# Blocks 6 and 7 normalised one by one, the d table's sines after blocks 8 and 9, and the last two blocks normalised after the first gate product

## The chip, the cores and the metric

The kernel runs on one NeuronCore of one Trainium2 chip. The metric is the device time of one execution in microseconds (us). A core has five engines that run their own instruction streams and wait for one another through semaphores: TensorE (PE in the profile, with its weight loads as PEld), VectorE (DVE), ScalarE (ACT), GpSimd (POOL) and SyncE (SP, which here only issues DMAs). Each engine takes its instructions in the order in which they were issued.

## The reference, cut to what matters

```python
def _A_ref(x, w_r, w_i):                       # x: 1 x 2048 x 512
    X = rfft2(x.astype(float32), axes=(-2, -1))
    return irfft2(X * (w_r + 1j * w_i), s=(2048, 512)).astype(bfloat16)

def _B_ref(x, w1, b1, w2, b2):                 # w1: 2048 x 1792, w2: 1792 x 2048
    h = _layernorm(x, axis=-1)
    u = gelu(einsum("bsd,sf->bdf", h, w1) + b1)
    return (einsum("bdf,fs->bds", u, w2) + b2).transpose(0, 2, 1)

g = sigmoid((x * gate_w).sum(-1, keepdims=True))
return g * _A_ref(x, A_w_r, A_w_i) + (1 - g) * _B_ref(x, B_w1, B_b1, B_w2, B_b2)
```

The same x goes into the gate, the spectral branch A and the MLP branch B, whose two products run over the 2048 tokens.

## The kernel before

The 2048 tokens are cut into NB = 16 blocks of 128 rows (block b lies in `xa` for b below 8, in `xb` above). Everything stands in one function; its order is written out by hand and is the order on each engine.

**The first stage.** Each block is normalised over its 512 features into `hn[:, b]`, and as soon as a block is ready TensorE multiplies it by the first 1024 columns of w1 (`mm1`, L275): 8 matmuls of 128x512 per block, one for each group `ft` of 128 columns, summed over the blocks in 8 PSUM banks. Blocks 0 to 11 are multiplied block by block, 8 `ft` each. The last four blocks are taken per `ft`: for the first `ft` blocks 12, 13, 14, 15, then a GELU (L354) on ScalarE, then the next `ft`, and so on. So a block that is late stops TensorE, which holds its matmuls in order.

**The steps of one block's normalisation:**

- `bstat(b)` (L246): bn_stats on DVE.
- `aggr(b0, b1)`: bn_aggr on DVE (L253), then 1e-5 added to the variance (L255), then rstd as a power of -0.5 on POOL (L258). Where `on_dve(b0)` holds (b0 up to NDVE = 6, or 14) L255 runs on DVE; elsewhere it runs on POOL, and POOL also makes the negated mean (L257).
- `norm(b0, b1)`: nmr = -mean * rstd, on DVE (L264) where `on_dve(b0)` holds, elsewhere on POOL (L262); then one ScalarE activation per block writes `hn` (L267).
- `norm_dve(b)` (L271): for blocks 0 to 5 DVE writes `hn` itself, with no nmr.

Blocks 6 and 7 are one pair before the change, as are 8 and 9, 10 and 11, 12 and 13, 14 and 15.

**The tables.** ScalarE also computes sines for the Fourier matrices: `sines_d()` makes the table TD of the feature axis from `md`, three activations (L198 twice, L201); `sines_a(0)` and `sines_a(1)` make TA of the token axis from `ma[0]` and `ma[1]`, four activations and one. Before each of them DVE masks the integer angles (`mask`, L195: 768 columns for md, 1024 for each `ma`). TD and TA go through DMA transposes on SP (L346, L348) and are first read by TensorE in `token` and `dpass` of branch A.

**Beside and after it.** `gprod(q)` (L279) is the gate's product of x and gate_w on DVE, four instructions of 2048 columns; after them DVE goes on with the radix-16 part of branch A's transform (L387 and on), and POOL makes row indices and gathers rows of the spectral weights (L182 to L189, L106). After the first stage TensorE takes the remaining 768 columns of w1 (L458), then w2 (L468), and `fill` deals these matmuls out between the Fourier matmuls of branch A by a clock kept in the program. That order is fixed when the kernel is built.

Of the kernel before, what the change touches and what calls it, by code (L numbers as in the profile page):

```python
# [18 lines left out]
NB = 16  # L19
# [3 lines left out]
NDVE = 6  # L23
# [20 lines left out]
def kernel(  # L44
# [57 lines left out]
    def gather_w(i):  # L102
        w = (A_w_r, A_w_i)[i]
        for o, src, idx in ((wn[:, i, 8:16].rearrange("p e l -> p (e l)"), w.rearrange("(c e) l -> c (e l)", e=8), 0),
                            (wn[:, i, 16], w, 1)):
            nc.gpsimd.indirect_dma_start(out=o, out_offset=None, in_=src,  # L106
                                         in_offset=bass.IndirectOffsetOnAxis(ap=widx[:, idx:idx + 1], axis=0))
# [51 lines left out]
    def iota(dst, pattern, base, cm=0):  # L159
        nc.gpsimd.iota(dst, pattern=pattern, base=base, channel_multiplier=cm,  # L160
                       allow_small_or_imprecise_dtypes=True)
# [19 lines left out]
    def gather_rows():  # L181
        gp = nc.gpsimd  # L182
        iota(widx[:, 0:1], [[0, 1]], 255, -2)
        gp.tensor_scalar(wf[:, 0:1], acol[:, 0:1], 63.5, 1016.0, op0=Alu.is_ge, op1=Alu.mult)
        gp.tensor_scalar(wf[:, 1:2], acol[:, 0:1], 0.5, -1024.0, op0=Alu.is_lt, op1=Alu.mult)
        gp.tensor_scalar(wf[:, 2:3], acol[:, 0:1], -16.0, 2048.0, op0=Alu.mult, op1=Alu.add)
        gp.tensor_add(wf[:, 0:1], wf[:, 0:1], wf[:, 1:2])
        gp.tensor_add(wf[:, 0:1], wf[:, 0:1], wf[:, 2:3])
        gp.tensor_copy(widx[:, 1:2], wf[:, 0:1])  # L189
# [4 lines left out]
    def mask(m, n):  # L194
        nc.vector.tensor_single_scalar(m, m, n - 1, op=Alu.bitwise_and)  # L195

    def nsin(dst, m, n):
        nc.scalar.activation(dst, m, ActF.Sin, bias=c_mpi, scale=2.0 * PI_IN / n)  # L198

    def psin(dst, m, n):  # L200
        nc.scalar.activation(dst, m, ActF.Sin, bias=c_pi, scale=-2.0 * PI_IN / n)  # L201
# [5 lines left out]
    def sines_d():  # L207
        nsin(TD[:, :, 1], md[:, 1], 1024)
        nsin(TD[:, :, 2], md[:, 0], 1024)
        psin(TD[:, :, 0], md[:, 0], 1024)  # L210

    def angles_a(v):
        mask(ma[v][:], 2048)
        if v == 0:
            mask(mc[:], 2048)

    def sines_a(v):
        if v == 1:
            nsin(TA[:, :, 1], ma[1][:], 2048)
        else:  # L220
            nsin(TA[:, :, 2], ma[0][:], 2048)
            psin(TA[:, :, 0], ma[0][:], 2048)
            nsin(TA[:, 0, 2, 0:1], mc[:], 2048)
            psin(TA[:, 0, 0, 0:1], mc[:], 2048)
# [20 lines left out]
    def bstat(b):  # L245
        nc.vector.bn_stats(out=stats[:, b, :], in_=xh[b // 8][:, b % 8, :])  # L246

    def on_dve(b):
        return b <= NDVE or b == NB - 2

    def aggr(b0, b1):
        for b in range(b0, b1):
            nc.vector.bn_aggr(out=mv[:, b, :], in_=stats[:, b, :])  # L253
        eng = nc.vector if on_dve(b0) else nc.gpsimd
        eng.tensor_scalar(mv[:, b0:b1, 1], mv[:, b0:b1, 1], 1e-5, 0.0, op0=Alu.add, op1=Alu.add)  # L255
        if not on_dve(b0):
            nc.gpsimd.tensor_scalar(nmr[:, b0:b1], mv[:, b0:b1, 0], -1.0, 0.0, op0=Alu.mult, op1=Alu.add)  # L257
        nc.gpsimd.tensor_tensor(rstd[:, b0:b1], mv[:, b0:b1, 1], c_mhalf.to_broadcast([P, b1 - b0]), op=Alu.pow)  # L258

    def norm(b0, b1):  # L260
        if not on_dve(b0):
            nc.gpsimd.tensor_mul(nmr[:, b0:b1], nmr[:, b0:b1], rstd[:, b0:b1])  # L262
        else:
            nc.vector.scalar_tensor_tensor(nmr[:, b0:b1], mv[:, b0:b1, 0], -1.0, rstd[:, b0:b1],  # L264
                                           op0=Alu.mult, op1=Alu.mult)
        for b in range(b0, b1):
            nc.scalar.activation(hn[:, b, :], xh[b // 8][:, b % 8, :], ActF.Identity,  # L267
                                 bias=nmr[:, b:b + 1], scale=rstd[:, b:b + 1])

    def norm_dve(b):  # L270
        nc.vector.tensor_scalar(hn[:, b, :], xh[0][:, b, :], mv[:, b, 0:1], rstd[:, b:b + 1],  # L271
                                op0=Alu.subtract, op1=Alu.mult)
# [5 lines left out]
    def gprod(q):  # L278
        nc.vector.tensor_mul(prod[q // 2][:, 4 * (q % 2):4 * (q % 2) + 4],  # L279
                             xh[q // 2][:, 4 * (q % 2):4 * (q % 2) + 4],  # L280
                             gwb[:, None, :].to_broadcast([P, 4, D]))
# [30 lines left out]
    for b in range(2, NDVE):  # L312
        bstat(b + 1)
        norm_dve(b)
        if b + 1 < NDVE:
            aggr(b + 1, b + 2)
    for b in range(NDVE, NB, 2):
        if b > NDVE:
            bstat(b)
        if b == NDVE + 2:  # L320
            norm(b - 2, b)
            sines_d()
        bstat(b + 1)
        aggr(b, b + 2)
        if b == NDVE:
            mask(md[:], 1024)
        if b == NB - 2:
            angles_a(1)
        if b > NDVE:
            norm(b, b + 2)  # L330
        if b == NB - 6:
            angles_a(0)
            sines_a(0)
# [3 lines left out]
            mm1(b, ft)  # L337
    for q in range(4):
        gprod(q)
    gather_rows()  # L340
    gather_w(0)
    gather_w(1)
# [452 lines left out]
    b = NB - 1  # L795
# [36 lines left out]
```

## Time and profile before

| What | us |
|---|---|
| time, median of 3 runs (lowest to highest) | 129.69 (128.85 to 129.98) |
| the profiled execution's own time | 128.63 |
| its span from first to last instruction | 126.7 |
| outside the span, 128.63 - 126.7 | 1.93 |
| PE busy | 122.3 |
| DVE busy | 111.6 |
| ACT busy | 89.7 |
| POOL busy | 39.6 |

The profile is one execution. A line of its timeline gives the start and the length of one instruction, or of several alike in a row (x2), counted in us from the span's start; in brackets the idle time of the engine just before it and what ended that. Two instructions in a row on one engine overlap a little, so the spacing from start to start is what an engine's order costs, and it is shorter than the length that stands there: two `hn` activations in a row are listed at 0.80 us each and start 0.70 us apart.

### The profile page before, as it was taken

Reading aid. Unit: us, or ns where it says so; the run is one execution under the profiler, and the core shown is the slowest. Engines: PE = TensorE matmul, PEld = TensorE weight load, DVE = VectorE, ACT = ScalarE, POOL = GpSimd, SP = SyncE. Lnnn points to the kernel's source line nnn. Section 1 sums busy time; section 2 is a strip of 40 time slices with the busy share of each in tenths; the row PEclk is TensorE's granted clock in tenths of the full one; section 3 lists DMA queues with packets and bytes.
Section 4 is the critical chain, followed back from the end, with each engine's and each line's share of the span. In section 5 each row is a group of like instructions: output and inputs, shape, how many; then the busy total and the mean of one; then the engine's idle time right before and its main releaser. Section 6 shows DMA issues by size and latency. Waiting matters only on the chain.

```text
span 126.7 us, 2074 instructions
## 1 busy us (share of the span) xinstructions
PE 122.3 (97%) x750; PEld 65.2 (51%) x750; DVE 111.6 (88%) x190; ACT 89.7 (71%) x137; POOL 39.6 (31%) x67
## 2 busy tenths in 40 slices
PE   6999999999999999999999999999999999999990
PEld 2244444444444576557764765477644444444480
DVE  4799998999999999999999999999999999993140
ACT  4391299999897699998994799229785599522420
POOL 7133288998887198000040000000000000261200
PEclk9999999999999999999999999999999999999998
DMA  3899999998899999999579206710021101269991
GB/s 95 268 327 379 368 374 352 292 309 262 206 276 121 320 290 293 290 287 291 143 220 294 65 0 190 228 42 0 0 79 50 41 3 41 83 82 201 175 224 29
DMA packets 34635, 24.05 MB, mean 190 GB/s; under 512 B 5536, under 2 KB 32032, under 8 KB 34624
## 3 DMA queue, kind: packets, MB, share of 16 engines
q1 hardware_dynamic: 32516, 21.02, 60.4%
q0 software_dynamic: 1936, 2.76, 13.0%
q8 instruction: 6, 0.10, 0.3%
q10 hardware_dynamic: 172, 0.13, 0.3%
q14 instruction: 5, 0.04, 0.1%
HBM read 19.15 MB, written 3.67 MB: 180 GB/s over the span
## 4 chain that ended last, share of the span: by engine, by line
PE 97%; DVE 0%; issue 0%
PE yb L468 36%; PE u L275 22%; PE u L458 16%; PE ivt L657 5%; PE ivd L673 3%; PE pw L240 3%; PE dp L525 3%; PE yb L800 2%; PE tok L516 2%; PE tok L517 2%; PE ivt L651 0%; PE tok L513 0%; DVE tbv L802 0%; DVE warm L145 0%; PE pb L239 0%
## 5 line engine op out<-in xcount | busy, mean ns | idle before, releaser
L468 PE MATMUL yb<-gl,w2t 128*128 128x512 bf16 x210 | 47.4, 379 | 0.0
L468 PEld LDWEIGHTS <-w2t 128*128 128x128 bf16 x210 | 20.2, 98 | 22.1
L275 PE MATMUL u<-hn,w1a 128*128 128x512 bf16 x128 | 28.5, 385 | 0.0
L458 PE MATMUL u<-hn,w1b 128*128 128x512 bf16 x96 | 23.3, 379 | 0.0
L448 ACT ACTIVATE tbv<-yb,ombb,omg 128x512 bf16<-128x512 f32 x15 | 11.6, 775 | 15.3 <-PE yb L468 15.1
L275 PEld LDWEIGHTS <-w1a 128*128 128x128 bf16 x128 | 12.7, 99 | 15.9 <-issue 1.5
L778 POOL DMA_DIRECT2D out_dram<-ap x3 | 4.0, 1528 | 49.2 <-DVE ap L773 45.3
L458 PEld LDWEIGHTS <-w1b 128*128 128x128 bf16 x96 | 9.0, 98 | 8.0
L286 ACT ACTIVATE junk<-prod 128x512 bf16<-128x512 bf16 x16 | 10.1, 631 | 0.3
L354 ACT ACTIVATE gl<-u,bcol 128x512 bf16<-128x512 f32 x14 | 9.2, 688 | 1.3 <-PE u L458 0.8
L629 ACT CAST R<-ivt 128x1024 bf16<-128x1024 f32 x8 | 7.8, 1038 | 2.3 <-PE ivt L657 2.3
L258 POOL TENSOR_TENSOR rstd<-mv,consts 128x2 f32<-128x2 f32 (+1 forms) x9 | 6.3, 703 | 8.1 <-DVE mv L255 8.0
L629 ACT CAST H<-ivd 128x1024 bf16<-128x1024 f32 x7 | 6.9, 1047 | 0.8 <-PE ivd L673 0.8
L787 DVE TENSOR_TENSOR tbv<-tbv,ap 128x512 bf16<-128x512 bf16 x3 | 1.3, 425 | 5.5 <-ACT tbv L448 5.5
L246 DVE BATCH_NORM_STATS2 stats<-xa 128x6 f32<-128x512 bf16 x8 | 5.5, 686 | 0.5 <-DMA xa<-in_A_x_dram 0.5
L267 ACT ACTIVATE hn<-xb,nmr,rstd 128x512 bf16<-128x512 bf16 x8 | 5.8, 802 | 0.0
L547 DVE TENSOR_TENSOR tatb<-PMA,wn 128x1024 bf16<-128x1024 bf16 x8 | 5.0, 690 | 0.2 <-issue 0.2
L246 DVE BATCH_NORM_STATS2 stats<-xb 128x6 f32<-128x512 bf16 x8 | 5.2, 676 | 0.0
L267 ACT ACTIVATE hn<-xa,nmr,rstd 128x512 bf16<-128x512 bf16 x2 | 1.5, 804 | 5.1 <-DVE nmr L264 5.1
L673 PEld LDWEIGHTS <-R 128*128 128x128 bf16 x64 | 3.8, 98 | 2.5 <-ACT R L629 2.5
L547 DVE TENSOR_TENSOR tatb<-PMB,wn 128x2048 bf16<-128x2048 bf16 x4 | 4.7, 1226 | 0.2
L518 ACT CAST ZA<-tok 128x1024 bf16<-128x1024 f32 x4 | 4.0, 1019 | 1.4 <-PE tok L517 1.3
(198 smaller groups left out, 225.8 us busy)
## 6 DMA issues: line engine op xcount, KB each, us to landing
w2t<-in_B_w_dram SPq DMA_DIRECT2D x8, 896.0 KB, 9.8
w1b<-in_B_w_dram SPq DMA_DIRECT2D x3, 1024.0 KB, 16.3
w1a<-in_B_w_dram SPq DMA_DIRECT2D x2, 1024.0 KB
out_dram<-tbv SPq DMA_DIRECT2D x14, 128.0 KB, 4.0
out_dram<-ap POOLq DMA_DIRECT2D x3, 512.0 KB, 6.8
w1a<-in_B_w_dram SPq DMA_DIRECT2D x4, 256.0 KB, 4.4
w1a<-in_B_w_dram SPq DMA_DIRECT2D x2, 512.0 KB, 8.0
xb<-in_A_x_dram SPq DMA_DIRECT2D x2, 512.0 KB, 7.3
```

The lines of the kernel that those rows point to most:

```text
L246: nc.vector.bn_stats(out=stats[:, b, :], in_=xh[b // 8][:, b % 8, :])
L267: nc.scalar.activation(hn[:, b, :], xh[b // 8][:, b % 8, :], ActF.Identity, bias=nmr[:, b:b + 1], scale=rstd[:, b:b + 1])
L275: nc.tensor.matmul(u1[ft], lhsT=w1a[b // 4][:, b % 4, ft * P:(ft + 1) * P], rhs=hn[:, b, :], start=(b == 0), stop=(b == NB - 1))
L286: nc.scalar.activation(junk[:], prod[b // 8][:, b % 8], ActF.Copy, accum_out=glog[:, b:b + 1])
L354: nc.scalar.activation(gl[:, ft, :], src, ActF.Gelu_apprx_tanh, bias=b1f[:, ft:ft + 1], scale=1.0)
L448: nc.scalar.activation(tbv[0][:, b], y[:], ActF.Identity, bias=gate["ombb2"][:, b:b + 1], scale=gate["omg"][:, b:b + 1])
L458: nc.tensor.matmul(u[:], lhsT=w1b[c][:, b, k * P:(k + 1) * P], rhs=hn[:, b, :], start=(b == 0), stop=(b == NB - 1))
L468: nc.tensor.matmul(y[:], lhsT=w2t[b // 2][:, ft, (b % 2) * P:(b % 2 + 1) * P], rhs=gl[:, ft, :], start=(ft == 0), stop=(ft == NFT - 1))
L547: mul(tt[:, i, :, r:r + n], PM[:, 2 * s:2 * s + 2, r:r + n], w[:, None].to_broadcast([P, 2, n, 256]))
L629: nc.scalar.copy(out, pr[:].rearrange("p h n -> p (h n)"))
L657: nc.tensor.matmul(o[:, 2 * v:2 * v + 2], lhsT=UV[:, 2 * v + c, r, par::2], rhs=TB[:, s, c:c + 2], start=(c == 0), stop=(c == 1))
L673: nc.tensor.matmul(pr[:, c, o * P:(o + 1) * P], lhsT=plane(par, cos), rhs=TI[:, lst, t], start=True, stop=True)
```

## The change

Blocks 6 and 7 are no longer a pair: the loop over the single blocks now also makes the factors of block 6, whose nmr comes from DVE; block 7 follows alone, with its factors on POOL. The mask of `md` moves on DVE behind the bn_aggr of blocks 8 and 9, and `sines_d()` moves on ScalarE behind `hn` of 8 and 9. The call `norm(14, 16)` moves out of the loop and stands behind `gprod(0)`; in ScalarE's order `sines_a(1)`, which came after `hn` of blocks 14 and 15, now comes before them.

```diff
     for b in range(2, NDVE):
         bstat(b + 1)
         norm_dve(b)
-        if b + 1 < NDVE:
-            aggr(b + 1, b + 2)
-    for b in range(NDVE, NB, 2):
-        if b > NDVE:
-            bstat(b)
-        if b == NDVE + 2:
-            norm(b - 2, b)
-            sines_d()
+        aggr(b + 1, b + 2)
+    bstat(NDVE + 1)
+    norm(NDVE, NDVE + 1)
+    aggr(NDVE + 1, NDVE + 2)
+    norm(NDVE + 1, NDVE + 2)
+    for b in range(NDVE + 2, NB, 2):
+        bstat(b)
         bstat(b + 1)
         aggr(b, b + 2)
-        if b == NDVE:
+        if b == NDVE + 2:
             mask(md[:], 1024)
         if b == NB - 2:
             angles_a(1)
-        if b > NDVE:
+        if b < NB - 2:
             norm(b, b + 2)
+        if b == NDVE + 2:
+            sines_d()
         if b == NB - 6:
             angles_a(0)
             sines_a(0)
...
     for q in range(4):
         gprod(q)
+        if q == 0:
+            norm(NB - 2, NB)
```

The orders that come out of it, on the three engines that change (bstat, aggr and hn with their blocks; TD, TA0 and TA1 are the sines):

| Engine | Before | After |
|---|---|---|
| DVE | bstat 7, aggr 6-7, mask md, bstat 8, nmr 6-7, bstat 9, aggr 8-9, ... | aggr 6, bstat 7, nmr 6, aggr 7, bstat 8, bstat 9, aggr 8-9, mask md, ... |
| DVE, later | aggr 14-15, mask ma1, nmr 14-15, gprod 0, 1, 2, 3 | aggr 14-15, mask ma1, gprod 0, nmr 14-15, gprod 1, 2, 3 |
| ACT | hn 6, 7, TD, hn 8 to 11, TA0, hn 12 to 15, TA1, GELUs | hn 6, 7, 8, 9, TD, hn 10, 11, TA0, hn 12, 13, TA1, hn 14, 15, GELUs |
| POOL | rstd 6-7, factors 8-9, ... | rstd 6, factors 7, factors 8-9, ... |

## The prediction

> **What bounds the kernel.** I read the page first: how much of the span TensorE is busy, and what the chain of waits is made of.
>
> ```profile
> span 126.7 us, 2074 instructions
> ...
> PE 97%; DVE 0%; issue 0%
> ```
>
> The chain that ended last is TensorE alone, without an idle piece in it worth a line. So a saving elsewhere buys nothing, and time can be gained only where TensorE waits. The timeline of TensorE from the end of the first stage (L275) comes next, where L458 follows, then two narrow cuts: at block 6, and at two ordinary matmuls.
>
> ```profile
> 33.15 3.62 PE L458 MATMUL u<-hn,w1b 128*128 128x512 bf16 x16
> ...
> 36.81 6.87 PE L458 MATMUL u<-hn,w1b 128*128 128x512 bf16 x31
> ```
> ```profile
> 15.58 0.68 PE L275 MATMUL u<-hn,w1a 128*128 128x512 bf16 x2
> ```
> ```profile
> 57.01 0.59 PE L458 MATMUL u<-hn,w1b 128*128 128x512 bf16 x2
> ```
>
> 31 matmuls from 36.81 to the next kind at 43.51 are 0.216 us each. Counting back from 33.15, the first matmul of block 6 (80 before the end of L275) is at 15.89, and the first of block 15 (29 before) at 26.89. Two ordinary matmuls take 0.59; the pair from 15.58 takes 0.68. That is the one wait of the stage: 0.09 us, at the last of block 5 and the first of block 6. It is all that the edit to blocks 6 and 7 can win.
>
> ScalarE's timeline says who was late there, and what room blocks 14 and 15 have.
>
> ```profile
> 15.03 1.52 ACT L267 ACTIVATE hn<-xa,nmr,rstd 128x512 bf16<-128x512 bf16 x2 [5.06 <-DVE nmr L264]
> 16.45 1.10 ACT L198 ACTIVATE TD<-md,consts 128x384 bf16<-128x384 int32 x2
> ...
> 17.97 2.92 ACT L267 ACTIVATE hn<-xb,nmr,rstd 128x512 bf16<-128x512 bf16 x4
> 20.79 1.13 ACT L198 ACTIVATE TA<-ma,consts 128x1024 bf16<-128x1024 int32 x1
> ...
> 23.24 2.92 ACT L267 ACTIVATE hn<-xb,nmr,rstd 128x512 bf16<-128x512 bf16 x4
> 26.06 1.14 ACT L198 ACTIVATE TA<-ma,consts 128x1024 bf16<-128x1024 int32 x1
> ```
>
> From 15.03 ScalarE has no gap: it is a second, full queue beside TensorE. `hn` 6 starts at 15.03, takes 0.80, and TensorE goes on at 15.89, 0.06 after its end. `hn` 15 starts 0.70 before 26.06, at 25.36, and is ready at 25.36 + 0.86 = 26.22; TensorE wants it at 26.89. The room is 0.67 us.
>
> Last, DVE and then POOL, which feed ScalarE. DVE is waited for at 14.83, and its mask at 17.11 matters for POOL.
>
> ```profile
> 12.34 0.41 DVE L271 TENSOR_SCALAR hn<-xa,mv,rstd 128x512 bf16<-128x512 bf16 x1
> ...
> 14.83 0.16 DVE L264 SCALAR_TENSOR_TENSOR nmr<-mv,rstd 128x2 f32<-128x2 f32 x1
> ...
> 17.11 0.66 DVE L195 TENSOR_SCALAR ma<-ma 128x1024 int32<-128x1024 int32 x1
> ```
> ```profile
> 17.17 0.65 POOL L262 TENSOR_TENSOR nmr<-nmr,rstd 128x2 f32<-128x2 f32 x1
> ...
> 19.14 0.20 POOL L262 TENSOR_TENSOR nmr<-nmr,rstd 128x2 f32<-128x2 f32 x1
> ```
>
> The same L262 takes 0.20 alone and 0.65 when it starts inside a mask (17.11 to 17.77): it ends 0.05 after the mask. A mask holds POOL up. Trainium skill, "SBUF — State Buffer", section "SBUF: two separate sides": VectorE in a two-port mode and GpSimd lock their shared port for a whole instruction, and whoever starts first keeps the other out. The trace agrees for L262, which lost to the mask.
>
> **The change, part by part.**
>
> *Block 6 alone.* DVE is unchanged up to L271 at 12.34. L253 follows 0.33 later (12.67), L255 0.21 after that (12.88, as from 11.32 to 11.53), bstat 7 at 12.95. rstd starts 0.23 after L255 and takes 0.55 (11.76 to 12.31 for the block before): 13.11 to 13.66. nmr on DVE 0.03 later, 13.69; `hn` 6 0.20 after that (14.83 to 15.03): 13.89, ready 14.75. The 0.09 wait goes; TensorE then wants block 15 at 26.80.
>
> *Block 7 alone.* L253 at 13.77, done 13.94; POOL starts 0.09 after the end of bn_aggr, its L257 0.33 after that and L258 another 0.16 (as at 15.81, 15.90, 16.23 and 16.39 for blocks 8 and 9), 0.55 for one column, and L262 from 15.15 to 15.35. `hn` 7 starts at about 15.4, ready 16.25; wanted eight matmuls after block 6, at 17.5. POOL's three more instructions cost nothing: blocks 8 and 9 stand behind them, as follows.
>
> *Mask of md.* bstat 8 and 9 at 13.87 and 14.45 (0.58 apart), bn_aggr at 15.04, the mask from 15.27 to about 15.85. POOL's L255 for 8 and 9 would start at 15.44, inside it. Held till about 15.95, then L257, L258 (0.70) from 16.19 and L262 from 16.97 to 17.16. The next mask, of ma0, starts 0.47 + 0.58 + 0.59 + 0.22 = 1.86 after the first, at 17.13 to 17.19: L262 starts some 0.2 before it. `hn` 8 then starts at 17.2. The delay from POOL to ScalarE is shown by no row (ScalarE never waited for POOL); from POOL or DVE to its neighbour it is 0.03 to 0.04, at most the 0.20 above. If the first mask did not hold POOL, `hn` 8 would be 0.5 earlier; if the second one catches L262, it is 0.7 later (below).
>
> *Sines of d behind 8 and 9.* ScalarE gains 15.03 - 13.89 = 1.14 at the start, and idles before `hn` 7 (14.6 to 15.4) and `hn` 8 (16.1 to 17.2), 1.9 in all, since TD, which filled that time, has been moved. From 17.2 on it is full again: two `hn` 1.41, TD 1.52 (16.45 to 17.97), so `hn` 10 starts at 20.12 against 17.97 + 1.41 = 19.38 before: **0.75 behind**. `hn` 10 to 13 are still ready over 0.8 before TensorE wants them.
>
> *norm(14, 16) moved.* On DVE nmr now comes after gprod 0, at 22.5 to 23.2 instead of 22.04 (its rstd may be held through gprod 0, 1.22 long); gprod 1 follows at 23.25 at the latest, where it was before, so the DVE queue behind it loses nothing, and ScalarE gets to `hn` 14 only after 26. What costs is the order on ScalarE: TA1 now runs before `hn` 14 and 15, 1.04 from start to start (20.79 to 21.83). `hn` 15 starts at 25.36 + 0.75 + 1.04 = 27.15, ready at 28.0; `hn` 14 at 27.3, wanted at 26.59. TensorE stops at block 14 for 0.7 and at block 15 for 0.5. Against 26.89 before it is **1.10 us late**.
>
> What is late next: the GELUs start after the table load at 29.25 (28.51 before) and need 0.635 each while TensorE now delivers one per 0.87 from 28.4; they have caught up by the sixth, and no PSUM bank is missed. From there TensorE has no slack in which to lose 1.10, and the whole program behind it moves. The transposes on SP (L346) are issued at 31.30, long after TD and TA in either order. Sum: 128.63 + 1.10 = 129.73 for the profiled execution. The median lies 1.06 above that execution; carried over as it is, **130.8**, with 130.3 (first mask holds nothing, +0.6) to 131.5.
>
> **The rivals.**
>
> *The second mask catches L262.* It decides on some 0.2 us of POOL's time. L262 then ends 0.05 after the mask's end at 17.8, `hn` 8 starts at 17.9, TensorE is 1.8 late: 131.5. For it: the 0.65 row. Against: by my starts L262 is first. By the lock rule of the Trainium skill, told above, whoever starts first wins; that is the forecast.
>
> *Not slower: TensorE is late anyway.* TensorE's first seven matmuls take 3.17, 0.43 apart, and it is at full pace only after 6 us. In an execution where that comes later, TensorE reaches block 15 later, while `hn` 15, paced by DVE, POOL and ScalarE, does not. If all of the 1.06 between profile and median lies there, the stop shrinks from 1.10 to 0.04: 129.73, the same as before; it decides as soon as the lateness reaches 1.1. Against: one trace shows no second pace, and 128.85 is a run near the profile. The Trainium skill, "TensorE: Matmul & The Clock Gate", Part 1 on the clock gate, says that the window that releases the clock runs free, so that the release moves from run to run; the trace shows one release, and cannot show that.
>
> *No stop at all.* `hn` 8 and all behind it would have to be 1.1 earlier than worked out, for which I see no row; then only the 0.09 is left: 129.6.
>
> *More than a stop.* Were TensorE to fall back to its first pace after idling and stay there 5 us as at the start, that would be 2.5 more, 133.3. The 0.09 wait had no such effect; a longer one is not in the trace.
>
> **Chances and range.** Forecast 0.41, second mask 0.28, TensorE late anyway 0.19, no stop 0.07, more than a stop 0.05. 129.6 to 131.9 leaves out the last, the lower half of no stop, and tails. One per cent, about what a measurement of this kernel can tell from no change, is 1.3 us: 128.4 to 131.0. Slower by more: 0.26 of the second mask, 0.05, and the upper 0.16 of the forecast, 0.47. Faster by more: 0.03, noise on the not slower cases, as only 0.09 can be won. Within: 0.50.
>
> **What would show it.** In the trace after: `hn` 6 at 13.9 and idle ScalarE before `hn` 7 and 8; `hn` 8 at 17.2 (17.9 is the second mask); TA1 before `hn` 14, `hn` 15 at 27.1; matmuls of block 14 and 15 at 27.3 and 28.0, L458 at 34.25. Wrong: L458 still at 33.1, or a gap in TensorE behind 34 that was not there.

## The result, and the profile after

| | before | after |
|---|---|---|
| median, lowest to highest of 22 runs each (us) | 128.81 (128.26 to 129.98) | 129.51 (129.23 to 129.96) |
| time of the profiled execution | 128.63 | 129.89 |
| its span | 126.7 | 128.1 |

The changed kernel is slower by 0.70 us, ratio 1.0052 (95% interval 1.0035 to 1.0069): slower, within one per cent, and 0.09 below the range. The 22 runs of before include the three that were known at the prediction (128.85, 129.98, 129.69); the median of the three stood 0.88 above that of all. A few of the runs that follow fell in a slower state of the core; medians and ratios leave them out.

The page of the changed kernel: the span and the two lines of the chain of waits, then TensorE's group of the first stage and ScalarE's `hn` group of blocks 8 to 15 (busy time, mean ns of one, then the idle time before them and what ended it):

```profile
span 128.1 us, 2078 instructions
...
PE 75%; ACT 9%; DVE 7%; POOL 3%; DMA 2%; issue 1%
...
L275 PE MATMUL u<-hn,w1a 128*128 128x512 bf16 x128 | 28.6, 383 | 1.0 <-ACT hn L267 1.0
...
L267 ACT ACTIVATE hn<-xb,nmr,rstd 128x512 bf16<-128x512 bf16 x8 | 6.0, 800 | 0.9 <-POOL nmr L262 0.9
```

TensorE was 97% of the chain and is 75%: the chain now leaves TensorE in the first stage and goes back through ScalarE, POOL and DVE to a load of x. TensorE has 1.0 us of idle time before L275, put down to `hn`. The timelines of TensorE, ScalarE and POOL show where:

```profile
27.22 0.38 PE L275 MATMUL u<-hn,w1a 128*128 128x512 bf16 x1 [0.62 <-ACT hn L267]
27.93 6.42 PE L275 MATMUL u<-hn,w1a 128*128 128x512 bf16 x29 [0.33 <-ACT hn L267]
34.18 1.03 PE L461 MATMUL u<-hn,w1b 128*128 128x512 bf16 x4
```
```profile
13.89 0.81 ACT L267 ACTIVATE hn<-xa,nmr,rstd 128x512 bf16<-128x512 bf16 x1 [3.92 <-DVE nmr L264]
15.37 0.81 ACT L267 ACTIVATE hn<-xa,nmr,rstd 128x512 bf16<-128x512 bf16 x1 [0.67 <-POOL nmr L262]
17.12 1.52 ACT L267 ACTIVATE hn<-xb,nmr,rstd 128x512 bf16<-128x512 bf16 x2 [0.93 <-POOL nmr L262]
18.55 1.10 ACT L198 ACTIVATE TD<-md,consts 128x384 bf16<-128x384 int32 x2
...
20.06 1.50 ACT L267 ACTIVATE hn<-xb,nmr,rstd 128x512 bf16<-128x512 bf16 x2
...
25.33 1.13 ACT L198 ACTIVATE TA<-ma,consts 128x1024 bf16<-128x1024 int32 x1
26.37 1.50 ACT L267 ACTIVATE hn<-xb,nmr,rstd 128x512 bf16<-128x512 bf16 x2
```
```profile
15.15 0.19 POOL L262 TENSOR_TENSOR nmr<-nmr,rstd 128x1 f32<-128x1 f32 x1
15.42 0.45 POOL L255 TENSOR_SCALAR mv<-mv 128x2 f32<-128x2 f32 x1
...
16.89 0.19 POOL L262 TENSOR_TENSOR nmr<-nmr,rstd 128x2 f32<-128x2 f32 x1
```

`hn` 14 is started at 26.37, behind TA1 at 25.33. TensorE makes a single matmul at 27.22 (block 14), waits again, and from 27.93 (block 15) runs without a break; the remaining w1 columns (L461, L458 before the change) start at 34.18 against 33.15. The matmul before it started at 26.22, so the two stops are 27.22 - 26.22 - 0.216 = 0.79 and 27.93 - 27.22 - 0.216 = 0.49, 1.28 together; the idle times in the brackets are shorter, since a matmul's listed 0.38 reaches into the next one's spacing. TensorE had been 0.25 earlier at block 6 (15.64 against 15.89), so 1.03 is left. ScalarE idles 0.67 before `hn` 7 and 0.93 before `hn` 8. On POOL L262 starts at 16.89, ahead of the mask of ma0 at 17.11, and takes 0.19; L255 at 15.42 meets the mask of md (15.25 to 15.78) and takes 0.45.

From the first matmul of the second stage to the last of all, every profiled execution took 89.95 or 89.96 us, start to start, where no matmul was added in between, whatever was changed in the first stage. So the start of L458 (L461 and so on in the edited kernels, named L458 below) reads the whole cost of the first stage.

### The profile page after: what moved, and what is told of

It reads as the page before. It is cut to its first block, busy times and chain, and to the rows that moved or that the text cites. A ratio compares the mean times of both kernels' runs of the same rounds, so it can differ in the third digit from the quotient of the medians.

```text
span 128.1 us, 2078 instructions
## 1 busy us (share of the span) xinstructions
PE 122.4 (96%) x750; PEld 65.2 (51%) x750; DVE 111.5 (87%) x190; ACT 89.8 (70%) x137; POOL 40.6 (32%) x71
## 4 chain that ended last, share of the span: by engine, by line
PE 75%; ACT 9%; DVE 7%; POOL 3%; DMA 2%; issue 1%
PE yb L471 35%; PE u L461 16%; PE u L275 5%; PE ivt L660 5%; ACT hn L267 4%; PE ivd L676 3%; PE dp L528 3%; POOL rstd L258 3%; PE yb L803 2%; DVE stats L246 2%; PE tok L520 2%; PE tok L519 2%; DVE hn L271 2%; ACT TA L198 2%; DMA xa<-in_A_x_dram 2%
## 5 line engine op out<-in xcount | busy, mean ns | idle before, releaser
L275 PE MATMUL u<-hn,w1a 128*128 128x512 bf16 x128 | 28.6, 383 | 1.0 <-ACT hn L267 1.0
L461 PE MATMUL u<-hn,w1b 128*128 128x512 bf16 x96 | 23.3, 379 | 0.0
L275 PEld LDWEIGHTS <-w1a 128*128 128x128 bf16 x128 | 12.7, 99 | 17.0 <-issue 2.7
L461 PEld LDWEIGHTS <-w1b 128*128 128x128 bf16 x96 | 9.0, 98 | 8.0
L258 POOL TENSOR_TENSOR rstd<-mv,consts 128x1 f32<-128x1 f32 (+1 forms) x10 | 6.5, 652 | 7.4 <-DVE mv L255 7.4
L676 PE MATMUL ivd<-TI,R 128*128 128x128 bf16 x64 | 4.9, 220 | 0.0
```

What stands on the lines that cost most here:

```text
L275: nc.tensor.matmul(u1[ft], lhsT=w1a[b // 4][:, b % 4, ft * P:(ft + 1) * P], rhs=hn[:, b, :], start=(b == 0), stop=(b == NB - 1))
L461: nc.tensor.matmul(u[:], lhsT=w1b[c][:, b, k * P:(k + 1) * P], rhs=hn[:, b, :], start=(b == 0), stop=(b == NB - 1))
L676: nc.tensor.matmul(pr[:, c, o * P:(o + 1) * P], lhsT=plane(par, cos), rhs=TI[:, lst, t], start=True, stop=True)
```

## The experiments

The theory after the result: the whole cost is ScalarE's order, in two parts that draw on the same 0.67 us of room (TD displaced, TA1 ahead of `hn` 14). Against it: the nmr behind the gate product, or a fixed cost of the new steps. Open too was why the medians differ by 0.70 and the traces by 1.03. Ratios are to the kernel before, timed beside each experiment.

**e1, e2, e3: ScalarE's order put back.** e1 puts `sines_a(1)` behind `norm(14, 16)`, e2 puts `sines_d()` ahead of `hn` 8 and 9, e3 does both.

```diff
# e1
-    sines_a(1)
...
         if q == 0:
             norm(NB - 2, NB)
+            sines_a(1)
# e2
+        if b == NDVE + 2:
+            sines_d()
         if b < NB - 2:
             norm(b, b + 2)
-        if b == NDVE + 2:
-            sines_d()
```

> The changed kernel with sines_a(1) put back behind hn 14 and 15 on ScalarE; nmr of 14 and 15 stays behind gprod 0. If ScalarE's order is the cause, hn 15 is ready 1.04 earlier than in the changed kernel (27.92 - 1.04 = 26.88) against 26.65 to 26.89 when TensorE wants it: the stop shrinks from 1.7 in all to at most 0.25, L458 starts at 33.15 instead of 34.18, and the median is that of before, ratio 0.998 to 1.002. If the nmr behind the first gate product is what is late, the stop stays at about 1.0 and the ratio at 1.005.

> The changed kernel with sines_d put back ahead of hn 8 and 9 on ScalarE, its mask left where the change put it. If ScalarE's order is the cause, TD fills the gap before hn 8 (from 16.1 to 17.6), hn 8 starts at 17.6, later than in the changed kernel, but hn 10 at 19.0 instead of 20.06, and hn 15 is ready at 26.87: again L458 at 33.15 and ratio 0.998 to 1.002. If only the place of TA1 matters, nothing is won: L458 at 34.2, ratio 1.005.

> Both orders on ScalarE put back; what stays of the change is blocks 6 and 7 taken singly, the later mask and the nmr behind gprod 0. hn 15 is ready at about 25.85, no stop at 14 or 15, and none at block 6: L458 at 32.9 to 33.06, that is 0.09 to 0.25 earlier than before, ratio 0.997 to 1.0. If the parts that stay cost something themselves (DVE or POOL behind), ratio 1.002 or more.

| | median (us) | ratio (95%) | first L458 (us) |
|---|---|---|---|
| e1 | 128.94 | 1.0004 (0.9982 to 1.0025) | 33.44 |
| e2 | 128.74 | 0.9997 (0.9980 to 1.0013) | 33.49 |
| e3 | 129.01 | 1.0003 (0.9978 to 1.0027) | 33.44 |

Either edit alone takes the cost away. ScalarE and TensorE of e1:

```profile
23.95 2.92 ACT L267 ACTIVATE hn<-xb,nmr,rstd 128x512 bf16<-128x512 bf16 x4
26.77 1.14 ACT L198 ACTIVATE TA<-ma,consts 128x1024 bf16<-128x1024 int32 x1
```
```profile
25.67 7.93 PE L275 MATMUL u<-hn,w1a 128*128 128x512 bf16 x36
33.44 1.24 PE L461 MATMUL u<-hn,w1b 128*128 128x512 bf16 x5
```

The four `hn` of 12 to 15 are one run again, and TensorE passes block 14 without idle time. The start of L458 is nevertheless 0.3 later than expected in e1 and e2, and 0.4 to 0.5 later in e3: in these executions TensorE came late to block 6 by itself (16.2 in all three, against 15.89). In e1 and e2 its matmuls were still 0.43 apart until 6.9, against 6.1 in before. In e3 the waits name loads: 0.8 us of TensorE on w1a and 1.3 us of DVE's bn_stats on x in the first 10 us. e3 had the fastest runs of the study (128.04, 128.15), but its median is that of before, so no version here is shown to beat it.

**e4 and e7: one move alone, in the kernel before.** e4 only moves `norm(14, 16)`, e7 only the mask and the sines of d.

```diff
# e4
-        if b > NDVE:
+        if NDVE < b < NB - 2:
             norm(b, b + 2)
...
         gprod(q)
+        if q == 0:
+            norm(NB - 2, NB)
# e7
             norm(b - 2, b)
-            sines_d()
...
-        if b == NDVE:
+        if b == NDVE + 2:
             mask(md[:], 1024)
...
         if b > NDVE:
             norm(b, b + 2)
+        if b == NDVE + 2:
+            sines_d()
```

> The kernel before with norm(14, 16) alone moved behind gprod 0, and so behind TA1 on ScalarE. hn 15 starts at 25.36 + 1.04 = 26.40 and is ready at 27.25, wanted at 26.89: TensorE 0.36 late, L458 at 33.5. In the time, if each run's own lateness of TensorE hides part of a stop, less: +0.2 us, ratio 1.001 to 1.002; if a stop costs the same in every run, +0.36, ratio 1.003.

> The kernel before with the mask and the sines of d alone moved behind blocks 8 and 9. hn 8 at 17.1, hn 10 at 20.06, 0.7 later than before, TA1 still behind hn 15, which is ready at 26.88: the 0.67 of room is used up, no stop or one under 0.25, L458 at 33.1 to 33.2, ratio 0.998 to 1.002. Neither move alone then costs 0.7; the two together do, since both draw on the same room. If the gap on ScalarE costs by itself, ratio 1.004.

e4: median 129.10, ratio 1.0032 (1.0012 to 1.0052). TensorE's timeline:

```profile
25.63 1.46 PE L275 MATMUL u<-hn,w1a 128*128 128x512 bf16 x6
27.28 6.42 PE L275 MATMUL u<-hn,w1a 128*128 128x512 bf16 x29 [0.20 <-ACT hn L267]
33.54 1.24 PE L460 MATMUL u<-hn,w1b 128*128 128x512 bf16 x5
```

One stop, of 0.36 at block 15, at 27.28 where 27.25 was expected, and L458 at 33.54 where 33.5 was. The time rose by the fixed reading of it (1.003), not the smaller one.

e7: median 128.94, ratio 1.0039 (1.0012 to 1.0067), L458 at 33.49. `hn` 8 started at 17.23 and `hn` 10 at 20.18, each about 0.12 later than expected. Expected was no stop or one under 0.25, L458 at 33.1 to 33.2 and a ratio of at most 1.002; none of the three held, and that was a miss. TensorE was 0.11 late at block 8, 0.19 at block 15, and 0.24 at a place that nobody had priced, the start of the fifth group. Its weight load shows it, beside the first GELU on ScalarE:

```profile
30.04 0.96 PEld L275 LDWEIGHTS <-w1a 128*128 128x128 bf16 x5 [0.35 <-issue]
```
```profile
29.30 0.69 ACT L355 ACTIVATE gl<-u,bcol 128x512 bf16<-128x512 f32 x1
```

The profile names no releaser there, but the matmuls of the fifth group (`ft` 1) write into the PSUM tile that the first GELU (`ft` 0) still reads. In before that GELU ended at 29.20 and the group started at 29.70; in e7 it ended at 29.99, and the group started at 30.04. TA1 stands between `hn` 15 and the GELUs there, so a late `hn` 15 makes the GELUs late as well. The three stops are 0.54; TensorE had been 0.21 earlier at block 6, and 0.34 is left. So the two moves alone cost 0.39 and 0.34 by the start of L458, against 1.03 together.

**e8: nmr ahead of the gate product again.** On DVE only; ScalarE's order is that of the change.

```diff
+    norm(NB - 2, NB)
     for q in range(4):
         gprod(q)
-        if q == 0:
-            norm(NB - 2, NB)
```

> The changed kernel with nmr of blocks 14 and 15 ahead of gprod 0 on DVE again, ScalarE's order unchanged (TA1 before hn 14). If ScalarE's order is all, nothing moves: hn 14 and 15 at 26.4 and 27.1, L458 at 34.2, ratio 1.005. If the wait behind the gate product costs, L458 is earlier than 34.0 and the ratio under 1.003.

Median 129.46, ratio 1.0058 (1.0027 to 1.0090), with both stops in place and L458 at 34.28:

```profile
27.32 0.38 PE L275 MATMUL u<-hn,w1a 128*128 128x512 bf16 x1 [0.38 <-ACT hn L267]
28.02 6.42 PE L275 MATMUL u<-hn,w1a 128*128 128x512 bf16 x29 [0.33 <-ACT hn L267]
```

The place behind the gate product costs nothing. In the changed kernel nmr ended at 22.6 on DVE, and ScalarE did not ask for it before 26.37.

**e5, e6, e9, e10: TensorE made late.** More warm-up matmuls ahead of block 0, in both kernels: four in e5 and e6, fourteen in e9 and e10.

```diff
-    for n in range(8):
+    for n in range(12):      # e5, e6;  range(22) in e9, e10
```

> The kernel before with four more warm-up matmuls on TensorE ahead of block 0 (0.43 each before the clock is up), so that TensorE is late in every run. Block 0 starts at about 6.5 instead of 4.8, block 6 at 16.9, block 15 at 27.9, after hn 15 (26.2): no stop, L458 at about 34.15, 1.0 later than before; the time rises by 0.6 to 1.0, ratio 1.005 to 1.008.

> The changed kernel with the same four matmuls. If the change sets a floor under block 15 (hn 15 ready at 27.92) that TensorE's own lateness hides, nothing is added to it: L458 at 34.15 to 34.2 as without them, ratio 1.005 to 1.008, equal to the kernel before with the same four within 0.1%. If the change costs a fixed 0.7 in every run, it adds up: 0.7 above the kernel before with the four, ratio 1.011 or more.

> The kernel before with fourteen more warm-up matmuls on TensorE instead of four: block 0 starts at about 8.3, when hn 0 to 2 are ready, block 15 at 29.7, well after hn 15 in either kernel, L458 at about 35.9. No stop anywhere in the first stage; time about 35.9 + 89.96 (from the first L458 to the last matmul, the same in every trace so far) + 5.2 to 5.9 = 131.0 to 131.8, ratio 1.017 to 1.023.

> The changed kernel with the same fourteen. If the change only sets a floor under blocks 14 and 15, it costs nothing here: no stop, L458 at about 35.9, and the time of the kernel before with the fourteen within 0.2 us. If it costs a fixed 0.7 in every run, it stands 0.7 above it, ratio 1.022 to 1.029.

e5: 129.19, ratio 1.0037 (1.0010 to 1.0065); e6: 129.80, ratio 1.0085 (1.0051 to 1.0118). This pair settles nothing. The four matmuls made TensorE late by only 0.5 in e5 (L458 at 33.65), and `hn` 6 was just as late there (15.52). In the profiled execution of e6 `hn` 6 itself was 0.9 late (14.79), so that the stop was there in full.

With fourteen, e9 took 130.86 (five runs), ratio 1.0155 (1.0100 to 1.0211), and e10 131.05 (six runs), ratio 1.0172 (1.0123 to 1.0222). TensorE's timelines, e9 first, then e10:

```profile
4.11 3.41 PE L240 MATMUL pw<-warm 128*128 128x512 bf16 x15
7.36 27.79 PE L275 MATMUL u<-hn,w1a 128*128 128x512 bf16 x128
```
```profile
4.20 4.15 PE L240 MATMUL pw<-warm 128*128 128x512 bf16 x15
8.19 27.79 PE L275 MATMUL u<-hn,w1a 128*128 128x512 bf16 x128
```

The medians are 0.19 apart, and their intervals are too wide to tell 0.7 from nothing; the traces can. The 128 matmuls take 27.79 in both: no stop at all in the changed kernel once TensorE comes late enough. So the change sets a floor under block 15 and adds no cost of its own to the first stage. L458 stood at 34.99 and 35.82, where 35.9 was expected in both. The same 15 warm-up matmuls took 3.41 in one and 4.15 in the other: TensorE reached its full pace at another moment, and that is the 0.83 between the two.

**e11, e12, e16: the same kernels profiled again.** The kernel before twice more, and the changed kernel once more; no edit.

> The kernel before, unchanged, for a second look. If the profiled execution of before was an early one, L458 stands at 33.3 to 33.7 here, as in the experiments that had no stop (33.43, 33.49, 33.64), later by TensorE's own pace or a late load in the first 9 us. If 33.15 is the rule, it stands at 33.15 again and the 0.33 between the traces' 1.03 and the medians' 0.70 has to lie after the last matmul.

> A third look at the kernel before, with the same two readings: L458 at 33.3 to 33.7, or at 33.15.

> The changed kernel unchanged, timed with these on one chip and looked at again. Its L458 at 34.18 to 34.3 (two looks at ScalarE's new order gave 34.18 and 34.28), ratio 1.0052 as before; if its floor is softer than the trace says, L458 before 34.0.

L458 started at 33.24 and 33.17 in the two of before, and at 34.23 in the changed one. The first reading, that the profile of before was an early one, fell: three executions lie within 0.09. In e12 TensorE waited for DVE's `hn` twice in the first 9 us and was at the same place at block 6, which stood at 15.89, 15.98 and 15.91 in the three: there `hn` 6 holds TensorE, however early it comes. e16: median 129.78 of 7 runs, ratio 1.0095 (1.0059 to 1.0131); 1.03 of 128.67 would be 1.0080.

**e13, e14, e15: a delay without the change.** Matmuls repeated at the start of the second stage, five on the kernel before, five on the changed one, ten on the kernel before. The sum stays the same, since each starts afresh.

```diff
             u = bank("u2")
+            for _ in range(5 if ft == FT1 else 0):
+                nc.tensor.matmul(u[:], lhsT=w1b[c][:, 0, k * P:(k + 1) * P], rhs=hn[:, 0, :], start=True, stop=True)
             for b in range(NB):
```

> The kernel before with five more matmuls on TensorE between the first stage and the second: the first L458 matmul of the first group is made five times more, each with a fresh start, so the sum is the same. That puts 5 x 0.216 = 1.08 us on TensorE, with no stop and nothing moved in the first stage: the last matmul at 124.2 to 124.3, as in the changed kernel. If what follows the last matmul does not care, +1.08 us, ratio 1.0084. If it is shorter by about 0.3 whenever TensorE is late against the loads and stores, +0.75, ratio 1.0058, as the change itself shows.

> The changed kernel with the same five: last matmul at about 125.2 to 125.3. If the end does not care, 1.08 above the changed kernel of the same call, ratio to before about 1.0136; if it gives back more the later TensorE is, 1.011.

> The kernel before with ten such matmuls, 2.16 us. If the end does not care, ratio 1.0168; if it gives back 0.3 once, 1.0143.

| | added (us) | median minus before, 128.67 (us) | ratio (95%) |
|---|---|---|---|
| e13 | 1.08 | 0.83 | 1.0077 (1.0046 to 1.0107) |
| e15 | 2.16 | 1.87 | 1.0142 (1.0119 to 1.0164) |
| e14, on the changed kernel | 1.08 | 1.80 | 1.0154 (1.0117 to 1.0191) |

By the medians 0.25 and 0.29 of a known delay came back, about the same for five and for ten; e13's interval still holds the full 1.08 (1.0084), e15's does not hold 2.16 (1.0168). e14 lies 0.69 above e16, the changed kernel timed beside it, where 1.08 was added. The end of the program shows a place for it. Shown are the last DVE instruction and the three last stores on SP (as one row, from the first issue to the end of the last): two rows of before, two of e13, and the stores of e9:

```profile
123.37 0.35 DVE L802 SCALAR_TENSOR_TENSOR tbv<-yb,omg,ap 128x128 bf16<-128x128 f32 x1 [0.43 <-PE yb L800]
```
```profile
122.31 2.00 SPq L804 DMA_DIRECT2D out_dram<-tbv  x3
```
```profile
124.59 0.35 DVE L804 SCALAR_TENSOR_TENSOR tbv<-yb,omg,ap 128x128 bf16<-128x128 f32 x1 [0.43 <-PE yb L802]
```
```profile
123.54 1.76 SPq L806 DMA_DIRECT2D out_dram<-tbv  x3
```
```profile
124.15 1.76 SPq L804 DMA_DIRECT2D out_dram<-tbv  x3
```

The stores take 2.00 in before and 1.76 in the two delayed kernels, and from the start of the last DVE instruction to the end of the execution it is 128.63 - 123.37 = 5.26 in before and 129.49 - 124.59 = 4.90 in e13. But the row for the changed kernel's profile is 2.35, and from 124.40 to 129.89 it is 5.49: in that execution nothing came back, and its time is 1.26 above, 0.23 more than TensorE's 1.03. Over all eighteen profiled executions this end lasts 4.90 to 5.68. It is shorter than 5.1 in two of the nine whose last DVE instruction starts before 124 (e5, e7), and in six of the nine in which it starts later, the exceptions being the changed kernel, e16 and e6. So a later TensorE often goes with a shorter end, but what makes the end short in one execution and long in the next was not found.

## Why the prediction was partly right, and where it failed

- *Block 6 alone, block 7 alone.* Right to a few hundredths: `hn` 6 at 13.89 (13.89 forecast), L262 for block 7 at 15.15, `hn` 7 at 15.37. The 0.09 wait at block 6 is gone: block 6 starts at 15.64, 0.25 earlier. The other 0.16 is no gain of the edit: in this execution TensorE reached its full pace earlier (5.8 against 6.1).
- *The masks.* Right. L255 was held by the first (0.45 instead of 0.22 at its shortest), L262 came before the second (16.89; forecast 16.97), `hn` 8 at 17.12 (17.2). So the rival of the second mask did not occur. The lock rule of the Trainium skill, "SBUF — State Buffer", section "SBUF: two separate sides", agrees with the first row: the mask that was already running held L255 up. The second row does not test it, since L262 had ended (17.08) when the mask began (17.11).
- *Sines of d.* Right: `hn` 10 at 20.06 (20.12), 0.69 behind before (0.75 forecast).
- *norm(14, 16) and TA1.* Right: matmuls of block 14 and 15 at 27.22 and 27.93 (27.3 and 28.0), L458 at 34.18 (34.25). e1 and e2 show that putting back either order is enough to undo it, e8 that the gate product plays no part. The term of 1.10 (stops of 1.2 less 0.09) measured 1.03 (stops of 1.28 less 0.25). On DVE, where no loss was forecast, the work behind the gate product even started 0.70 earlier (25.95 against 26.65); TensorE does not wait for it, so it bought nothing.
- *What is late next.* Right: no new gap between 34 and the last matmul, 89.96 in both traces. The PSUM tile behind the GELUs, priced there as not missed, is what the third stop of e7, 0.24, is put down to.
- *Carrying over to the median: this step failed.* The prediction put "The median lies 1.06 above that execution; carried over as it is, 130.8". That 1.06 came from the median of three runs. Over 22 runs it is 0.18, and 128.63 + 0.18 + 1.10 = 129.91. The same 1.06 stands in the lower end, 129.6, which was the time with no stop at all: 128.63 - 0.09 + 1.06. With runs that spread over 1.13, the lower end should have been worked out from the profiled execution's own sum, 129.73, less the bounds of its terms, and not from an offset median.
- *The rest, 129.91 to 129.51.* 0.07 is the difference of 1.10 and 1.03. About 0.33 more lies between the traces' 1.03 and the medians' 0.70. TensorE's own lateness, the rival that was priced for it, does not carry it. The mechanism exists (e9, e10), but `hn` 6 holds block 6 in the kernel before: five executions with its first stage (before, e11, e12, e13, e15, the added matmuls counted as L458) have L458 at 33.15 to 33.39, 33.25 in the mean, and three with the changed one (the changed kernel, e14, e16) at 34.18 to 34.31, 34.24 in the mean. So TensorE's cost is 1.0 there too. The delays in e13 to e15 came back by 0.25 to 0.3 without the change, which fits an end that is shorter when TensorE is later. Against a settled story stand the profile of the changed kernel, with a long end, and e16, whose interval lies at 0.76 us and above. This stays open.
- *More than a stop.* Did not occur: after 0.62 and 0.33 us of idle time the matmuls kept their spacing of 0.216.

## What to carry to other kernels

Where one engine is the whole chain, look at the next fullest queue and write down, for each consumer, by how much its input is early; two moves that each overdraw that room by a little (0.39 and 0.34 late here) can together cost far more (1.03), since they draw on the same 0.67 us. Follow a late item one step further as well: here the GELUs behind it, and the PSUM tile that they free. In this kernel, filling ScalarE's idle time with work that is due late (the sines of d while `hn` 7 and 8 were being prepared) was worth more than starting its first urgent item 1.1 us earlier and idling 1.6 us after it. And make a forecast against the profiled execution, with a median of three runs as a bound and not as an offset.

## What the runs showed of the hardware that was not expected

- TensorE's change to full pace moved between executions: the 15 warm-up matmuls took 3.41 in e9 and 4.15 in e10. Matmuls were 0.43 apart until about 4.0 us in e9, 5.8 in e10, 6.1 in before and 6.9 in e1, and 0.216 apart after that. The Trainium skill, "TensorE: Matmul & The Clock Gate", Part 1 on the clock gate, says that the window which releases the clock runs free; these rows agree that the moment moves, and cannot show the window. Its effect on this kernel was small up to 6.1, as block 6 waits for `hn` 6 in before; in e1 and e2, at 6.9, TensorE was 0.3 late at block 6.
- The last three stores took 1.76 to 2.42 us on SP over the eighteen profiled executions, with the last DVE instruction always 1.05 or 1.06 after the start of the first. The end of an execution varied by 0.78 with them (4.90 to 5.68), while the start of L458 varied by 0.24 in the five executions with the first stage of before. So for this kernel the end is as much a source of differences between runs as the work.
